# Transposing q and k by DMA instead of on TensorE, in a fused attention and two-MLP kernel

## The chip, the cores and the metric

The kernel runs on one core of one Trainium2 chip. The metric is the device time of one execution in microseconds (us). Each version is timed in several runs; besides, one execution is recorded by the hardware profiler, and the rows below come from that one.

## What is computed

Inputs q, k and v have the shape (4, 8, 576, 64): batch, heads, sequence, head dimension, all float32. Attention is local: each chunk of 64 tokens attends to itself alone. The result, 2304 tokens of 512 features, goes through two MLPs.

```python
q_c = q.reshape(B, H, nc, 64, D)          # the same for k and v, nc = 9
scores = scale * q_c @ k_c^T
attn = exp(scores - max(scores)); attn = attn / (sum(attn) + 1e-9)
x = (attn @ v_c) laid out as (2304, 512)
h = x @ w_in                              # 512 -> 2048
g = max(h, 0) + alpha * min(h, 0)
x = g @ w_out                             # 2048 -> 512
out = ((x @ w_a) * (x @ w_b)) @ w_o       # 512 -> 1536 -> 512
```

The weights arrive as 64-bit floats; the kernel reads them as pairs of 32-bit integers and unpacks them itself. For precision every matmul of the MLPs is done as three, with each operand split into a high and a low float32r part (`three`, L314).

## The kernel before

**Tiles and stages.** The 2304 tokens are 18 units of 128 tokens (a unit is two chunks of all eight heads). They are grouped in five blocks, of 512, 256, 512, 512 and 512 tokens (`sizes`, L52), so units 0 to 3, 4 and 5, 6 to 9, 10 to 13 and 14 to 17. First comes the attention of block 0, in an order written out by hand (`order1`, L584). Then a loop over the blocks (L596) runs the first MLP: 16 hidden steps j per block, each a first-layer product `s1` into a PSUM bank psh, three passes of ScalarE and two of VectorE for the PReLU and the split (`prelu`), and a second-layer product `s2` into four accumulators acc. The second-layer product of a step is issued two steps later (`pend`, `flush(2)`). In block 0 the weights of the first MLP are also loaded, unpacked and split, a few units of work ahead (`prelu_unpacking`, L354; `w_dma`, L174). In the last block the weights of the second MLP follow. Then comes the second MLP over all blocks (L642).

**Attention under the MLP.** While block b goes through the first MLP, the attention of block b+1 is computed, in steps that `att_steps` (L459) returns as pairs (slot, step). Each hidden step has two slots: 2j comes behind the first-layer product, 2j+1 behind the second-layer product that is then due. `advance` (L600) runs all steps whose slot has come. All engines work through their instructions in the order in which they are issued.

For one unit the steps are:
- `load_qk` and `load_v` (L210, L214): DMAs on SP's queue that bring q, k and v with tokens on partitions, into tiles of the pool wp (72 tiles of 128x512; the split weights of the first MLP hold 64 of them).
- `att_T` (L227): four 128x128 transposes of k and four of q on TensorE into two PSUM banks psT, and two evictions by ScalarE into kT and qT (L234).
- `att_S` (L237): the scores, 32 small matmuls; `att_M` (L251): maximum and subtraction on VectorE.
- `soften`: exponential on ScalarE (L266), the sums and the division on VectorE (L268).
- `att_PT` (L277): four transposes of the softmax into psP, and an eviction by ScalarE.
- `att_O` (L286): the product with v, 32 small matmuls, split by ScalarE and VectorE into the next block's xh and xl.

For the blocks of four units, the steps are turn(w), multiply(w), soften(w) in turn, spread evenly over the slots 0 to 29: turn at 0, 7, 14, 21, 27, multiply at 3, 9, 16, 23, 29, soften at 5, 12, 18, 25. A turn transposes q and k of unit w, starts the loads of the next unit's q and k, and transposes the softmax of unit w-1. A multiply does the scores of unit w and the v product of unit w-1. For block 1 (units 4 and 5, under block 0) the slots are written out (L516).

**Shared buffers.** PSUM has four banks for psh, psT, psP, scores and v products together (`ps_p`), and four accumulators. The pool sp, three buffers with the tag stg, holds raw weights, and the tiles in which finished blocks go to and come back from DRAM (xs, xr).

Of the kernel before, what the change touches and what calls it, by code (L numbers as in the profile page):

```python
# [8 lines left out]
F32 = mybir.dt.float32  # L9
F32R = mybir.dt.float32r  # L10
I32 = mybir.dt.int32
U16 = mybir.dt.uint16
AF = mybir.ActivationFunctionType
# [5 lines left out]
def chunk_attention_prelu_mlp_bilinear_mlp(  # L19
# [17 lines left out]
    nc = tc.nc  # L37
    P = 128
    B, H, S, D = q.shape
    NT, DM = out.shape  # L40
# [5 lines left out]
    KD = DM // P  # L46
    J1 = F1 // P
    J2 = F2 // P
    NB = 512
    SCALE = 1.0 / float(D) ** 0.5  # L50

    sizes = [NB] + ([NT % NB] if NT % NB else []) + [NB] * (NT // NB - 1)  # L52
# [9 lines left out]
    sp = ctx.enter_context(tc.tile_pool(name="sp", bufs=3))  # L62
    st = ctx.enter_context(tc.tile_pool(name="st", bufs=4))
    dr = ctx.enter_context(tc.tile_pool(name="dr", bufs=1, space=bass.MemoryType.DRAM))
# [3 lines left out]
    def bank(nm="ps"):  # L68
        return ps_p.tile([P, DM], F32, tag="ps", name=nm)
# [5 lines left out]
    def wtile(name, dt=F32R):  # L75
        return wp.tile([P, DM], dt, tag="w", name=name)
# [88 lines left out]
    def weave(*chains):  # L165


        live, later = [], [iter(c) for c in chains]
        while live or later:
            if later:  # L170
                live.append(later.pop(0))
            live = [c for c in live if next(c, None) is not None]
# [16 lines left out]
    att = {}  # L189

    def runs(t, n):
        done = 0
        while done < n:
            b, s = divmod(t + done, S)
            step = min(n - done, S - s)
            yield done, step, b, s
            done += step

    def half(i):
        return slice(i * CH, (i + 1) * CH)  # L200

    def load(nm, u):
        a = att[nm, u] = wtile(f"{nm}{u}", F32)
        for off, n, b, s in runs(u * P, P):
            nc.sync.dma_start(
                out=a[off:off + n].rearrange("p (h d) -> p h d", h=H),
                in_={"q": q, "k": k, "v": v}[nm][b, :, s:s + n, :].rearrange("h p d -> p h d"),
            )

    def load_qk(u):  # L210
        load("k", u)
        load("q", u)

    def load_v(u):  # L214
        load("v", u)

    n_early = [0]

    def att_bank(u, nm):

        if u < sizes[0] // P:
            n_early[0] += 1
            if n_early[0] % 2:
                return acc_p.tile([P, DM], F32, tag="acc", name=nm)
        return bank(nm)

    def att_T(u, nms="kq"):  # L227
        for nm in nms:
            src = att.pop((nm, u))
            ps = att_bank(u, "psT")  # L230
            for g in range(KD):
                nc.tensor.transpose(ps[:, g * P:(g + 1) * P], src[:, g * P:(g + 1) * P], ident)  # L232
            t = wtile(f"{nm}T{u}", F32)
            nc.scalar.activation(out=t, in_=ps, func=AF.Copy)  # L234
            att[nm + "T", u] = lambda r, g, c, t=t: t[r, half(2 * g + c)]

    def att_S(u, pss=None):  # L237
        qT, kT = att.pop(("qT", u)), att.pop(("kT", u))
        pss = pss or [att_bank(u, "psS") for _ in range(2)]
        for y in range(2):  # L240
            for c in range(2):
                for e in range(2):
                    for x in (e, 1 - e):
                        i = half(e), 2 * x + y, c
                        nc.tensor.matmul(  # L245
                            out=pss[e][half(x), half(2 * y + c)], lhsT=qT(*i), rhs=kT(*i),
                            start=True, stop=True,
                        )
        att["s", u] = pss
# [15 lines left out]
    def att_X(u):  # L265
        nc.scalar.activation(out=att["e", u], in_=att["e", u], func=AF.Exp, scale=SCALE)  # L266
# [10 lines left out]
    def att_PT(u):  # L277
        e_ = att.pop(("e", u))
        ps = att_bank(u, "psP")
        for g in range(KD):  # L280
            nc.tensor.transpose(ps[:, g * P:(g + 1) * P], e_[:, g * P:(g + 1) * P], ident)  # L281
        t = wtile(f"eT{u}", F32)
        nc.scalar.activation(out=t, in_=ps, func=AF.Copy)  # L283
        att["eT", u] = t

    def att_O(u, xh, xl, col, pss=None):  # L286
        eT, v_ = att.pop(("eT", u)), att.pop(("v", u))
        pss = pss or [att_bank(u, "psO") for _ in range(2)]
        for g in range(KD):
            x, y = divmod(g, 2)  # L290
            for c in range(2):
                for e in (c, 1 - c):
                    nc.tensor.matmul(  # L293
                        out=pss[c][half(e), half(g)], lhsT=v_[half(c), half(2 * g + e)],
                        rhs=eT[half(c), half(4 * e + 2 * y + x)], start=True, stop=True,
                    )
        cols = [slice(col + c * CH, col + (c + 1) * CH) for c in range(2)]
        return [
            (xh[:, :, f], xl[:, :, f], ps[:, :KD * CH].rearrange("p (g i) -> p g i", g=KD))
            for f, ps in zip(cols, pss)  # L300
        ]

    def each(fn, parts):
        for part in parts:
            fn(*part)


    def xtiles(nm):
        return (
            xp.tile([P, KD, NB], F32R, tag="xh", name=nm + "h"),  # L310
            xp.tile([P, KD, NB], F32R, tag="xl", name=nm + "l"),
        )
# [138 lines left out]
    NU = NT // P  # L451
# [7 lines left out]
    def att_steps(b, x):  # L459

        t0, n = blocks[b]
        us = range(t0 // P, (t0 + n) // P)

        def turn(w):
            for u in us[w:w + 1]:
                att_T(u)
                if u + 1 < NU:
                    load_qk(u + 1)  # L470
            for u in us[max(w - 1, 0):w]:
                att_PT(u)
            return lambda: None

        def multiply(w):
            pss = [bank("psSO") for _ in range(2)]
            now, before = us[w:w + 1], us[max(w - 1, 0):w]
            for u in now:
                att_S(u, [ps[:, :KD * CH] for ps in pss])
            o = []  # L480
            for u in before:
                o += att_O(u, *x, u * P - t0, [ps[:, KD * CH:] for ps in pss])
                if u + 2 < NU:
                    load_v(u + 2)
            each(to_hi, o)

            def then():
                for u in now:
                    att_M(u)
                each(to_lo, o)  # L490

            return then

        def soften(u):
            att_X(u)
            return lambda: weave(att_N(u))

        def both(product):
            pss = [bank("psSO") for _ in range(2)]
            return [product(u, [ps[:, i * KD * CH:(i + 1) * KD * CH] for ps in pss]) for i, u in enumerate(us)]  # L500

        def both_S():
            both(att_S)
            return lambda: att_M(us[0])

        def both_O():
            o = sum(both(lambda u, pss: att_O(u, *x, u * P - t0, pss)), [])
            each(to_hi, o)
            for u in us:
                load_v(u + 2)  # L510
            return lambda: each(to_lo, o)

        def only(fn):
            return lambda: fn() and None or (lambda: None)

        if b == 1:  # L516
            u0, u1 = us
            return [
                (8, only(lambda: att_T(u0))),
                (10, only(lambda: (att_T(u1), load_qk(u1 + 1)))),  # L520
                (14, both_S),
                (16, lambda: lambda: att_M(u1)),
                (18, lambda: soften(u0)),
                (20, lambda: soften(u1)),
                (24, only(lambda: [att_PT(u) for u in us])),
                (27, both_O),
            ]
        steps = []
        for w in range(len(us) + 1):
            steps += [lambda w=w: turn(w), lambda w=w: multiply(w)]  # L530
            steps += [lambda u=u: soften(u) for u in us[w:w + 1]]
        last = 2 * J1 - 3
        return [(-(-last * i // (len(steps) - 1)), s) for i, s in enumerate(steps)]

    with tc.manual_schedule():
        n0 = sizes[0] // P
# [12 lines left out]
        x = xtiles("x")  # L549
# [46 lines left out]
        for b, (t0, n) in enumerate(blocks):  # L596
            nxt = xtiles("x")
            steps = att_steps(b + 1, nxt) if b + 1 < NBLK else []
# [11 lines left out]
            for j in range(J1):  # L610
# [5 lines left out]
                h = h0[0][:, :n] if not (b or j) else s1(j, x, n)  # L616
                if b == 0:
                    g = prelu_unpacking(j, h, lambda: w_dma(min(2 * j + 9, NU1)), lambda: advance(2 * j), settle)
                else:
                    rest = advance(2 * j)  # L620
                    g = prelu(j, h)
# [17 lines left out]
            x = nxt  # L639
        flush(0)  # L640

        for i, b in enumerate(order2):  # L642
            n = sizes[b]
            for j in range(J2):
                want = NU1 + max(3 * (j + 2), 20 + 2 * j)
                c = s3(j, x, n)
# [14 lines left out]
                if i + 1 < NBLK:  # L661
                    if j == J2 - 3:
                        nxt = xtiles("y")
                        halves = list(reload(order2[i + 1]))
# [3 lines left out]
            x = nxt  # L668
# [31 lines left out]
```

## Time and profile before

| what | value |
|---|---|
| runs, median | 912.65 us |
| runs, lowest and highest | 912.55, 913.15 us |
| the profiled execution's own time | 912.5 us |
| its span in the profile | 910.7 us |
| mean granted TensorE clock | 0.996 of full |
| TensorE (matmul) busy | 898.5 us, 99% |
| VectorE busy | 403.3 us, 44% |
| ScalarE busy | 339.4 us, 37% |

The span is the time from the first to the last recorded instruction; the rest of the profiled execution's time, 1.8 us, lies around it. Matmuls are pipelined and their recorded ends are modelled: two matmuls in a row overlap in the record, so what one costs is read from start to start. A row of the timeline is the start, the duration, the engine, the line of the kernel, the operation, the output and inputs by the program's names, the shape and the count.

### The profile page before, as it was taken

Reading aid. Unit: us, or ns where it says so; the run is one execution under the profiler, and the core shown is the slowest. Engines: PE = TensorE matmul, PEld = TensorE weight load, DVE = VectorE, ACT = ScalarE, POOL = GpSimd, SP = SyncE. Lnnn points to the kernel's source line nnn. Section 1 sums busy time; section 2 is a strip of 40 time slices with the busy share of each in tenths; the row PEclk is TensorE's granted clock in tenths of the full one; section 3 lists DMA queues with packets and bytes.
Section 4 is the critical chain, followed back from the end, with each engine's and each line's share of the span. In section 5 each row is a group of like instructions: output and inputs, shape, how many; then the busy total and the mean of one; then the engine's idle time right before and its main releaser. Section 6 shows DMA issues by size and latency. Waiting matters only on the chain.

```text
span 910.7 us, 13047 instructions
## 1 busy us (share of the span) xinstructions
PE 898.5 (99%) x5426; PEld 756.9 (83%) x5426; DVE 403.3 (44%) x762; ACT 339.4 (37%) x636; POOL 0.7 (0%) x6
## 2 busy tenths in 40 slices
PE   7999999999999999999999999999999999999998
PEld 6878899988888888888888888888888888888897
DVE  5999955443444343368856653111221122111222
ACT  5677654443433343356644432111211122111211
POOL 0000000000000000000000000000000000000000
PEclk9999999999999999999999999999999999999999
DMA  8685432221111110154424420200020002000100
GB/s 209 207 262 179 140 100 52 59 59 35 36 36 59 35 24 2 44 187 139 139 70 140 134 74 13 80 0 1 1 93 1 0 1 70 1 1 0 47 2 23
DMA packets 89098, 62.70 MB, mean 69 GB/s; under 512 B 59856, under 2 KB 81872, under 8 KB 89040
## 3 DMA queue, kind: packets, MB, share of 16 engines
q1 hardware_dynamic: 88752, 61.62, 22.8%
q8 instruction: 42, 0.69, 0.3%
q10 hardware_dynamic: 288, 0.26, 0.1%
q14 instruction: 16, 0.13, 0.1%
HBM read 53.49 MB, written 8.39 MB: 68 GB/s over the span
## 4 chain that ended last, share of the span: by engine, by line
PE 92%; DVE 5%; ACT 2%; issue 1%; POOLq 0%; ACTq 0%; POOL 0%; DVEq 0%
PE psh L317 52%; PE acc L317 36%; PE psT L232 1%; DVE wx L136 1%; PE psSO L245 1%; PE psP L281 1%; PE psSO L293 1%; DVE wz L128 1%; DVE wz L133 1%; DVE gl L82 0%; DVE sm L271 0%; DVE e L275 0%; PE warm L555 0%; DVE e L260 0%; DVE mx L258 0%
## 5 line engine op out<-in xcount | busy, mean ns | idle before, releaser
L393 DVE TENSOR_TENSOR b_sb<-psh,b_sb 128x512 f32<-128x512 f32 (+1 forms) x60 | 38.3, 638 | 273.2 <-PE psh L317 273.2
L337 DVE SCALAR_TENSOR_TENSOR pos<-neg,nalpha_sb,pos 128x512 f32<-128x512 f32 (+1 forms) x80 | 55.6, 695 | 116.4 <-ACT pos L336 116.2
L391 ACT ACTIVATE b_sb<-psh 128x512 f32<-128x512 f32 (+1 forms) x60 | 33.1, 552 | 167.9 <-PE psh L317 167.9
L79 ACT ACTIVATE ch<-b_sb 128x512 fp32r<-128x512 f32 (+1 forms) x60 | 35.3, 589 | 153.9 <-DVE b_sb L393 153.9
L335 ACT ACTIVATE neg<-psh 128x512 f32<-128x512 f32 (+1 forms) x80 | 44.1, 551 | 79.0 <-PE psh L317 79.0
L82 DVE TENSOR_TENSOR gl<-pos,gh 128x512 fp32r<-128x512 f32 (+1 forms) x80 | 51.0, 638 | 43.5 <-ACT gh L79 43.5
L79 ACT ACTIVATE gh<-pos 128x512 fp32r<-128x512 f32 (+1 forms) x80 | 47.3, 591 | 61.5 <-DVE pos L337 61.5
L82 DVE TENSOR_TENSOR cl<-b_sb,ch 128x512 fp32r<-128x512 f32 (+1 forms) x60 | 38.3, 639 | 39.3 <-ACT ch L79 39.3
L136 DVE SCALAR_TENSOR_TENSOR wx<-wx,wz 128x512 int32<-128x512 int32 x68 | 46.8, 688 | 4.9 <-ACT wx L124 1.0
L336 ACT ACTIVATE pos<-psh 128x512 f32<-128x512 f32 (+1 forms) x80 | 44.2, 552 | 0.0
L124 ACT ACTIVATE wx<-raw 128x512 f32<-128x512 f32 x68 | 42.7, 670 | 3.5 <-DMA raw<-in_moe_w_b_dram 3.4
L128 DVE TENSOR_SCALAR wz<-raw 128x512 uint16<-128x512 uint16 x68 | 29.7, 461 | 2.6 <-DMA raw<-in_moe_w_b_dram 2.6
L133 DVE TENSOR_SCALAR wz<-raw 128x512 uint16<-128x512 uint16 x68 | 30.9, 454 | 0.0
L234 ACT ACTIVATE kT<-psT 128x512 f32<-128x512 f32 x18 | 10.7, 594 | 20.1 <-PE psT L232 20.1
L79 ACT ACTIVATE xh<-psSO 128x256 fp32r<-128x256 f32 x28 | 9.1, 381 | 17.1 <-PE psSO L293 17.1
L266 ACT ACTIVATE e<-e 128x512 f32<-128x512 f32 x18 | 11.2, 623 | 10.4 <-DVE e L260 10.4
L281 PE MATMUL psP<-ident,e 128*128 128x128 f32 x72 | 11.6, 287 | 3.3 <-ACT eT L283 1.7
L258 DVE TENSOR_REDUCE mx<-psSO 128x4 f32<-128x256 f32 x28 | 10.5, 416 | 5.2 <-ACT xh L79 5.2
L275 DVE TENSOR_TENSOR e<-e,rc 128x512 f32<-128x512 f32 x18 | 12.4, 691 | 0.6
L271 DVE TENSOR_REDUCE sm<-e 128x8 f32<-128x512 f32 x18 | 12.2, 680 | 1.0 <-ACT e L266 0.8
L281 PEld LDWEIGHTS psP<-ident,e 128*128 128x128 f32 x72 | 8.5, 145 | 4.9 <-ACT eT L283 1.8
L232 PE MATMUL psT<-ident,q 128*128 128x128 f32 x72 | 11.2, 280 | 1.3 <-issue 1.3
(729 smaller groups left out, 2535.4 us busy)
## 6 DMA issues: line engine op xcount, KB each, us to landing
raw<-in_moe_w_out_dram SPq DMA_DIRECT2D x28, 512.0 KB, 3.5
raw<-in_moe_w_in_dram SPq DMA_DIRECT2D x16, 512.0 KB, 4.8
raw<-in_moe_w_b_dram SPq DMA_DIRECT2D x12, 512.0 KB, 4.9
raw<-in_moe_w_a_dram SPq DMA_DIRECT2D x12, 512.0 KB, 3.5
k<-in_k_dram SPq DMA_DIRECT2D x16, 256.0 KB, 3.8
q<-in_q_dram SPq DMA_DIRECT2D x16, 256.0 KB, 3.2
v<-in_v_dram SPq DMA_DIRECT2D x16, 256.0 KB, 3.3
out_dram<-os SPq DMA_DIRECT2D x8, 512.0 KB, 2.8
```

Source lines behind the costliest of these rows:

```text
L79: nc.scalar.activation(out=hi, in_=src, func=AF.Copy)
L82: nc.vector.tensor_tensor(out=lo, in0=src, in1=hi.bitcast(F32), op=ALU.subtract)
L124: return nc.scalar.activation(out=x.bitcast(F32), in_=hw.bitcast(F32), func=AF.Copy, scale=2.0 ** -112)
L128: yield nc.vector.tensor_scalar(out=z2[:, :, 0], in0=h2[:, :, 1], scalar1=13, scalar2=None, op0=ALU.logical_shift_right)
L133: yield nc.vector.tensor_scalar(out=z2[:, :, 1], in0=h2[:, :, 3], scalar1=1 << 15, scalar2=None, op0=ALU.bitwise_and)
L136: yield nc.vector.scalar_tensor_tensor(out=x, in0=x, scalar=3, in1=z, op0=ALU.logical_shift_left, op1=ALU.bitwise_or)
L317: nc.tensor.matmul(out=ps, lhsT=a, rhs=b, start=(i == 0 and first), stop=(i == n_i - 1 and a is wl))
L335: nc.scalar.activation(out=neg, in_=h, func=AF.Relu, scale=-1.0)
L336: yield nc.scalar.activation(out=pos, in_=h, func=AF.Relu)
L337: yield nc.vector.scalar_tensor_tensor(out=pos, in0=neg, scalar=nalpha_sb[:, j:j + 1], in1=pos, op0=ALU.mult, op1=ALU.add)
L391: nc.scalar.activation(out=b_sb, in_=pb, func=AF.Copy)
L393: nc.vector.tensor_tensor(out=b_sb, in0=pa, in1=b_sb, op=ALU.mult)
```

## The change

q and k of units 6 to 17 no longer go through TensorE. Their tiles are loaded as before, but earlier, and mostly into stg buffers (`load_kq`). ScalarE copies each tile as 16-bit integers so that the low and the high halves of all 512 floats are set apart, 512 of each per token (`halves`), and SP stores this to a DRAM tile of 128 tokens x 2 x 512 (`apart`). Then SP issues a transposing DMA, which reads that tile as 256 rows of 512 16-bit elements and writes kT or qT with features on partitions; low and high halves of a float land next to each other, so the result is the float32 tile that the scores read (`turned`, `turn_qk`). The evictions of psT go with the transposes. The even spread of steps is replaced by slots written out for each kind of step: m (multiply), s (soften), p (softmax transposes), l (load), a (apart), t (turn by DMA). One list is for the block of 256 tokens as the running one, the other for 512. In the pairs under l, a and t the second number is the unit counted from the first of the block whose attention is being computed, so 4 and more belong to the block after it. Units 0 to 5 are transposed on TensorE as before.

```diff
+    def load_kq(u, staged=True):
+        att["kq", u] = a = pair(f"kq{u}", staged)
+        for off, n, b, s in runs(u * P, P):
+            for i, src in enumerate((k, q)):
+                nc.sync.dma_start(
+                    out=a[i][off:off + n].rearrange("p (h d) -> p h d", h=H),
+                    in_=src[b, :, s:s + n, :].rearrange("h p d -> p h d"),
+                )
...
+    def halves(src, dst, nm):
+
+        d = dst.bitcast(U16).rearrange("p (t f) -> p t f", t=2)
+        nc.scalar.activation(out=d, in_=src.bitcast(U16).rearrange("p (f t) -> p t f", t=2), func=AF.Copy)
+        rows = dr.tile([P, 2, DM], U16, name=f"rows{nm}")
+        nc.sync.dma_start(out=rows, in_=d)
+        return rows
+
+    def turned(rows, nm):
+        t = wtile(nm, F32)
+        nc.sync.dma_start_transpose(
+            out=t.bitcast(U16).rearrange("p (g r) -> p g r", g=KD), in_=rows.rearrange("p t f -> (p t) f")
+        )
+        return t
+
+    def apart(u, staged=True):
+        a, d = att.pop(("kq", u)), pair("kqd", staged)
+        att["rows", u] = [halves(a[i], d[i], f"{nm}{u}") for i, nm in enumerate("kq")]
+
+    def turn_qk(u):
+        for nm, rows in zip("kq", att.pop(("rows", u))):
+            t = turned(rows, f"{nm}T{u}")
+            att[nm + "T", u] = lambda r, g, c, t=t: t[r, half(2 * g + c)]
...
-        def turn(w):
-            for u in us[w:w + 1]:
-                att_T(u)
-                if u + 1 < NU:
-                    load_qk(u + 1)
-            for u in us[max(w - 1, 0):w]:
-                att_PT(u)
-            return lambda: None
...
         if b == 1:
             u0, u1 = us
             return [
-                (8, only(lambda: att_T(u0))),
-                (10, only(lambda: (att_T(u1), load_qk(u1 + 1)))),
+                (8, only(att_T, u0)),
+                (10, only(att_T, u1)),
+                (10, only(load_kq, u1 + 1, False)),
                 (14, both_S),
                 (16, lambda: lambda: att_M(u1)),
                 (18, lambda: soften(u0)),
                 (20, lambda: soften(u1)),
-                (24, only(lambda: [att_PT(u) for u in us])),
-                (27, both_O),
+                (21, only(apart, u1 + 1, False)),
+                (24, only(att_PT, u0)),
+                (24, only(att_PT, u1)),
+                (24, only(turn_qk, u1 + 1)),
+                (25, only(load_kq, u1 + 2)),
+                (27, lambda: both_O(us)),
+                (28, only(apart, u1 + 2)),
+                (29, only(load_kq, u1 + 3)),
+                (30, only(turn_qk, u1 + 2)),
             ]
-        steps = []
-        for w in range(len(us) + 1):
-            steps += [lambda w=w: turn(w), lambda w=w: multiply(w)]
-            steps += [lambda u=u: soften(u) for u in us[w:w + 1]]
-        last = 2 * J1 - 3
-        return [(-(-last * i // (len(steps) - 1)), s) for i, s in enumerate(steps)]
+        u = us[0]
+        if sizes[b - 1] < NB:
+            S_, lag = {
+                "m": (0, 7, 14, 21, 28), "s": (2, 9, 16, 23), "p": (6, 13, 20, 27),
+                "l": ((4, 3), (11, 4), (18, 5), (29, 6)), "a": ((1, 2), (8, 3), (15, 4), (24, 5)), "t": ((4, 2), (11, 3), (25, 4), (29, 5)),
+            }, 1
+        else:
+            S_, lag = {
+                "m": (0, 6, 12, 18, 28), "s": (2, 8, 14, 20), "p": (5, 11, 17, 27),
+                "l": ((3, 3), (9, 4), (15, 5), (24, 6)), "a": ((1, 2), (7, 3), (15, 4), (23, 5)), "t": ((3, 2), (13, 3), (21, 4), (29, 5)),
+            }, 1
...
```

## Rows read from the trace of the kernel before

**Rows 1.** The page: span, and busy time of each engine
```profile
span 910.7 us, 13047 instructions
...
PE 898.5 (99%) x5426; PEld 756.9 (83%) x5426; DVE 403.3 (44%) x762; ACT 339.4 (37%) x636; POOL 0.7 (0%) x6
```

**Rows 2.** The chain of waits from 110 to 380 us, shares of that stretch by line
```profile
by line: PE psh L317 43.8%; PE acc L317 42.3%; PE psT L232 3.4%; PE psSO L245 2.8%; PE psSO L293 2.3%; PE psP L281 2.1%; issue 0.4%; DVE pos L337 0.4%; ACT gh L79 0.3%; DVE gl L82 0.3%; DVE e L275 0.3%; DVE e L260 0.2%; DVE mx L258 0.2%; AC
```

**Rows 3.** Windows by stage: us, busy us by engine, clock, DMA share, GB/s
```profile
36.00:117.00 81.00, 79.55 (x477) 64.99 (x476) 77.21 (x156) 58.87 (x108) 0.00 (x0) 1.00 0.64 194
117.00:177.60 60.60, 59.98 (x690) 57.24 (x689) 32.16 (x76) 30.30 (x78) 0.00 (x0) 1.00 0.32 77
177.60:273.20 95.60, 95.60 (x690) 79.34 (x690) 38.36 (x74) 39.22 (x75) 0.00 (x0) 1.00 0.17 40
273.20:371.40 98.20, 98.20 (x690) 80.90 (x689) 39.16 (x74) 39.33 (x75) 0.00 (x0) 1.00 0.11 28
```

**Rows 4.** Timeline of TensorE, a turn with k, q and softmax, 512-token stage
```profile
198.28 0.39 PE L317 MATMUL acc<-gh,wo1l 128*128 128x512 f32 x1
198.51 0.60 PE L232 MATMUL psT<-ident,k 128*128 128x128 f32 x4
...
199.74 0.48 PE L317 MATMUL psh<-xh,wi4h 128*128 128x512 f32 x1
```

**Rows 5.** Timeline of TensorE, a turn with the softmax alone, 512-token stage
```profile
260.74 0.39 PE L317 MATMUL acc<-gh,wo11l 128*128 128x512 f32 x1
260.97 0.60 PE L281 MATMUL psP<-ident,e 128*128 128x128 f32 x4
261.32 0.48 PE L317 MATMUL psh<-xh,wi14h 128*128 128x512 f32 x1
```

**Rows 6.** Timeline of TensorE, a turn with k and q alone, 512-token stage
```profile
275.69 0.39 PE L317 MATMUL psh<-xh,wi0l 128*128 128x512 f32 x1
...
276.71 0.48 PE L317 MATMUL acc<-gh,wo14h 128*128 128x512 f32 x1
277.02 0.40 PE L317 MATMUL acc<-gl,wo14h 128*128 128x512 f32 x1
```

**Rows 7.** Timeline of TensorE, three turns in the 256-token stage
```profile
132.70 0.28 PE L317 MATMUL acc<-gh,wo1l 128*128 128x256 f32 x1
...
134.05 0.36 PE L317 MATMUL psh<-xh,wi4h 128*128 128x256 f32 x1
...
145.37 0.28 PE L317 MATMUL psh<-xh,wi7l 128*128 128x256 f32 x1
...
146.86 0.63 PE L281 MATMUL psP<-ident,e 128*128 128x128 f32 x4 [0.34 <-ACT kT L234]
147.24 0.36 PE L317 MATMUL acc<-gh,wo5h 128*128 128x256 f32 x1
...
170.24 0.28 PE L317 MATMUL acc<-gh,wo11l 128*128 128x256 f32 x1
...
170.89 0.36 PE L317 MATMUL psh<-xh,wi14h 128*128 128x256 f32 x1
```

**Rows 8.** Groups of ScalarE instructions, shapes apart: count, busy us, mean ns, idle before
```profile
L124 ACT ACTIVATE wx<-raw 128x512 f32<-128x512 f32 x68 | 42.7, 670 | 3.5 <-DMA raw<-in_moe_w_b_dram 3.4
...
L234 ACT ACTIVATE kT<-psT 128x512 f32<-128x512 f32 x18 | 10.7, 594 | 20.1 <-PE psT L232 20.1
...
L79 ACT ACTIVATE yh<-xr 128x1024 fp32r<-128x1024 f32 x6 | 6.3, 1044 | 0.0
```

**Rows 9.** DMA issues by line: count, KB each, median us to landing
```profile
x2d<-xs SPq DMA_DIRECT2D x2, 256.0 KB, 2.3
xr<-x2d SPq DMA_DIRECT2D x2, 256.0 KB, 3.9
```

**Rows 10.** DMA queue of SP: packets, MB, share of 16 engines
```profile
q1 hardware_dynamic: 88752, 61.62, 22.8%
```

**Rows 11.** Timeline of SP's DMA issues near the end of the first block
```profile
97.99 6.59 SPq L100 DMA_DIRECT2D raw<-in_moe_w_out_dram  x3
```

More of the change, by code (lines that the diff above doesn't have):

```diff
@@ L212, in load_qk, with pair @@
         load("q", u)
+    def pair(nm, staged):
+        if not staged:
+            return [wtile(nm, F32) for _ in range(2)]
+        a = sp.tile([P, 2, DM], F32, tag="stg", name=nm)
+        return [a[:, i] for i in range(2)]
+    def load_kq(u, staged=True):
[6 more added lines that the diff above has]
+                )
     def load_v(u):
         load("v", u)
+    def halves(src, dst, nm):
[17 more added lines that the diff above has]
+            att[nm + "T", u] = lambda r, g, c, t=t: t[r, half(2 * g + c)]
     n_early = [0]
@@ L464, in att_steps, with multiply @@
         us = range(t0 // P, (t0 + n) // P)
-        def turn(w):
-            for u in us[w:w + 1]:
-                att_T(u)
-                if u + 1 < NU:
-                    load_qk(u + 1)
-            for u in us[max(w - 1, 0):w]:
-                att_PT(u)
-            return lambda: None
-        def multiply(w):
+        def multiply(w, lag):
             pss = [bank("psSO") for _ in range(2)]
-            now, before = us[w:w + 1], us[max(w - 1, 0):w]
+            now, before = us[w:w + 1], us[max(w - lag, 0):max(w - lag + 1, 0)]
             for u in now:
@@ L496, in soften, with both @@
             return lambda: weave(att_N(u))
-        def both(product):
+        def both(product, us):
             pss = [bank("psSO") for _ in range(2)]
@@ L502, in both_S, with both_O, nothing, only @@
         def both_S():
-            both(att_S)
+            both(att_S, us)
             return lambda: att_M(us[0])
-        def both_O():
-            o = sum(both(lambda u, pss: att_O(u, *x, u * P - t0, pss)), [])
+        def both_O(us):
+            o = sum(both(lambda u, pss: att_O(u, *x, u * P - t0, pss), us), [])
             each(to_hi, o)
             for u in us:
-                load_v(u + 2)
+                if u + 2 < NU:
+                    load_v(u + 2)
             return lambda: each(to_lo, o)
-        def only(fn):
-            return lambda: fn() and None or (lambda: None)
+        def nothing():
+            pass
+        def only(fn, *a):
+            def step():
+                if a[0] < NU:
+                    fn(*a)
+                return nothing
+            return step
         if b == 1:
@@ L524, in att_steps @@
                 (20, lambda: soften(u1)),
-                (24, only(lambda: [att_PT(u) for u in us])),
-                (27, both_O),
-            ]
-        steps = []
-        for w in range(len(us) + 1):
-            steps += [lambda w=w: turn(w), lambda w=w: multiply(w)]
-            steps += [lambda u=u: soften(u) for u in us[w:w + 1]]
-        last = 2 * J1 - 3
-        return [(-(-last * i // (len(steps) - 1)), s) for i, s in enumerate(steps)]
+                (21, only(apart, u1 + 1, False)),
[7 more added lines that the diff above has]
+                (30, only(turn_qk, u1 + 2)),
+            ]
+        u = us[0]
[9 more added lines that the diff above has]
+            }, 1
+        steps = [(slot, lambda w=w: multiply(w, lag)) for w, slot in enumerate(S_["m"])]
+        steps += [(slot, lambda w=w: soften(us[w])) for w, slot in enumerate(S_["s"])]
+        steps += [(slot, only(att_PT, us[w])) for w, slot in enumerate(S_["p"])]
+        for i, fn in enumerate((load_kq, apart, turn_qk)):
+            steps += [(slot, only(fn, u + n)) for slot, n in S_["lat"[i]]]
+        return sorted(steps, key=lambda s: s[0])
     with tc.manual_schedule():
```

## The prediction, made before the changed kernel ran

> **What bounds the kernel now.** I read the page's busy times first: TensorE is busy for 99% of the span, VectorE and ScalarE under half of it [rows 1]. A matmul's end is modelled, so this alone proves little. The chain of waits does more: cut to the stretch in which the touched attention work lies, it is nearly all TensorE, with the psT transposes on it at 3.4%, and VectorE and ScalarE at tenths of a per cent [rows 2]. The windows by stage say the same: behind the first block TensorE is never idle for long, ScalarE works about 40 to 50% of the time and VectorE as much [rows 3]. In the first block it is otherwise: VectorE is busy 77.2 of 81.0 us there and ScalarE 58.9. So time taken out of TensorE's stream in the three later stages should come off the end, and what is added elsewhere is free until TensorE has to wait for it.
>
> **What the change takes out of TensorE's stream.** For each of the units 6 to 17 the eight 128x128 transposes of k and q go. How long each takes is read from starts, since the durations overlap. In a 512-token stage the step in which k, q and the softmax (psP) are transposed runs from the last acc matmul at 198.28 to the next psh matmul at 199.74: 1.46 us [rows 4]. The same step with psP alone, which is what the change leaves, takes 260.74 to 261.32: 0.58 us [rows 5]. The difference is 0.88 us. Where a stage opens with k and q alone, 275.69 to 276.71 is 1.02 us, less the 0.23 that one matmul takes there anyway (the spacing in rows 4 and 5 of undisturbed 512-column matmuls, seen as 0.23 from 198.28 to 198.51), so 0.79; the next matmul follows after 0.31 in place of 0.23, so 0.87 goes in all [rows 6]. In the 256-token stage the psP step alone is 170.24 to 170.89, 0.65 us; with k and q it is 1.35 us (132.70 to 134.05), and, where psP also waited for a bank that kT's eviction had to free, 1.87 us (145.37 to 147.24) [rows 7]. So 0.70 there and 1.22 where it waited; the third such step waited as well, for the softmax itself, and I take 1.2. The last wait should not come back: before, psP came two slots behind the softmax steps, after, three or four.
> The sum: stage of 256 tokens, 0.87 + 0.70 + 1.22 + 1.20 = 4.0 us; two stages of 512, each 0.87 + 3 x 0.88 = 3.5 us. Together **11.0 us**. As a cross-check, 3.4% of the 270 us of [rows 2] is 9.2 us, without the changeovers and the two waits.
>
> **What stays, and what moves.** Scores, softmax, psP and the products with v are issued as often as before. Their slots move by three at most (a slot is half a hidden step: 2.9 us in the first block, 81.0 / 28, since its slots 4 to 31 lie in that window, 1.9 in the 256-token stage, 60.6 / 32, and 3.0 in the others [rows 3]). The psP eviction still has a slot between it and the product that reads it, at the least 1.9 us against one eviction of 0.59 (kT's, of the same shape [rows 8]). The last product moves from slot 29 to 28, so the next block's input is no later. I cost all this at nothing; its cover is TensorE's own stream, and if that fails the price is the wait of 0.3 us seen in [rows 7], a few times over. PSUM gets easier, since two banks per unit aren't asked for.
>
> **ScalarE.** Two evictions of 0.594 us per unit go; two copies over 1024 16-bit elements per partition come. No row shows a 16-bit copy of that form. The nearest are the 128x1024 f32 copies, 1.04 us [rows 8]; the bounds are 0.6 (as if 512 elements) and 1.3 (twice the longest 512-wide row, 0.67). At 1.04 ScalarE gains 0.9 us per unit, 11 us over 12 units, in stages where it idles for half the time or more [rows 3]. A pair holds the three prelu passes behind it on ScalarE's queue for 2.1 us, and so the psh bank; the second-layer product that reads them comes two hidden steps later, four slots, 7.6 us in the narrow stage and 12 in the wide ones. Nothing, then. In the first block two pairs come (units 6 and 7), where ScalarE is busy for 73%: 4.2 us spread over two steps of 5.8, with the same two steps as cover. Nothing again, but the cover is thinner.
>
> **The SP queue.** Per unit come two stores of 256 KB and two transposing loads of 256 KB; k and q loads move to a unit or more earlier, into the shared staging buffers. The store's row is the 256 KB x2d store, 2.3 us, and for a load out of the kernel's own DRAM tile the 256 KB xr load, 3.9 us [rows 9]. A transposing DMA stands in no row. Low end: 2.3 us. High end: if every 16-bit element were a packet of its own, 131072 packets at the queue's mean of 37 ns (22.8% of 16 x 910.7 us over 88752 packets [rows 10]) over 16 engines, 306 us each. I take 3.9, because the xr row is the same queue, the same direction, the same bytes and the same kind of source; so **7.8 us a pair** if they run one behind the other. The queue waits for ScalarE's copies at the stores, and for the stores at the transposes; behind it stand the next k, q and v loads, which have a unit's time.
> What matters is the lead from issue to the scores that read the pair, counted in slots: 20 us for unit 6 (seven slots of 2.9 to the block's end), 16 for 7 (one such, and seven of 1.89), 19 for 8 and 9 (ten of 1.89), 13.2 for 10 (slot 25 to the next stage's start, seven of 1.89), 15 for 13 and 17 (five of 3.0), over 20 for the rest. 7.8 us is under all of them, so the transposes cost nothing: the sum stays at 11.0.
> A row says 3.9 us for this size. The Trainium skill, "VectorE: DVE Perf Modes", The three transpose paths, gives 1309 ns for the DMA crossbar on one 128x128 block of 16-bit data; a tile here has eight such blocks, by my estimate 10.5 us and 21 us a pair if they follow one another, which would not be hidden and would make the whole about 19 us slower than before. The Trainium skill, "DMA: Bandwidth & Descriptors", Latency and other measured facts, has 261 GB/s for a transposing DMA, an estimated 1.0 us per tile, which would leave the sum as it is. No run shown here decides between them.
>
> **The rivals.**
> Slow transposes, the one on the other side: each takes 10 us or more, some 2.6 times the xr row, so 20 us a pair. Then the scores wait where the lead is short: unit 10 for 6.8 us, 13 and 17 for 5 each, 7 for 4, 8 and 9 for 1.1 each, in all 23 us, which less 11.0 ends at 912.5 + 12 = **924.5 us**. It decides from about 17.5 us a pair on, where these waits reach 11 us. For it: the operation is unseen, and a store must land before it. Against it: the rings are used for 11 to 32% of the time there [rows 3]. The Trainium skill's 1309 ns (VectorE: DVE Perf Modes, The three transpose paths) speaks for it too.
> A jam at the end of the first block: unit 6's transposes stand on the queue just ahead of the last raw weights (three w_out and w_in loads around 98 to 105 us, already spaced by waits [rows 11]), and its copies want two more working tiles when the weight tiles fill the pool. Unpacking is in order on engines that are 73 to 95% busy there [rows 3]. If the raw tiles come some 16 us late (two pairs at 7.8) against two steps of cover, 11.6 us, about 5 us of the gain goes: **906.5 us**.
> No gain: the freed time is refilled by waits of the same size on moved steps or late copies, or the change doesn't in fact take the transposes off TensorE's path: **912.5 us**. For it: only the change of slots, which no row prices. Against it: the chain.
>
> **How the numbers follow.** The profiled execution took 912.5 us, 0.15 under the median of the runs; 912.5 - 11.0 = **901.5 us**. Forecast 0.67, its own range 899 to 904.5 (the missing waits and a cheaper changeover one way, a few waits of 0.3 us and one bank held by ScalarE the other). Jam 0.12, slow transposes 0.16, no gain 0.05. The range of 8 in 10 runs from 899 to 911, over the forecast and the jam; the slow case and the no gain case are left out with two in ten. 0.2% is 1.8 us, about what this measurement can tell from no change. Faster: forecast and jam, 0.79; same: most of the no gain case, 0.04; slower: the slow transposes and the rest, 0.17.
>
> **What the profile after would show.** Right: psT transposes 24 each of k and q (units 0 to 5) in place of 72; no L232 work after 120 us; the 256-token stage 4 us shorter, each of the two after it 3.5 us; no wait of TensorE for a DMA-written kT or qT; ScalarE's copies near 1.04 us; transposes landing in 3 to 5 us. Wrong: scores that wait for kT or qT, above all units 10, 13 and 17 (slow transposes); ScalarE or VectorE waiting for raw, or the first block longer than before (jam); stages as long as before with new releasers in TensorE's waits (no gain). The prediction falls if a transposing DMA takes over some 8.5 us, or if ScalarE's copy takes several times 1.04.

## The result and the profile after

The changed kernel takes **901.57 us** (901.50 to 901.70), the kernel before, timed alongside it, 912.60: a ratio of 0.9878, 95% interval 0.9866 to 0.9891, or 11.0 us less.

The page after: busy time of each engine. TensorE is still at 99%, of a span of 899.7 us, and ScalarE has grown by 10.5 us (339.4 in [rows 1]).

```profile
PE 889.1 (99%) x5330; PEld 747.5 (83%) x5330; DVE 402.7 (45%) x762; ACT 349.9 (39%) x636; POOL 0.7 (0%) x6
```

The windows by stage after (us of the window, busy us and count for TensorE, its weight loads, VectorE, ScalarE, GpSimd, then granted clock, DMA share, GB/s). The stages are cut at the first psh matmul of each block, as in [rows 3].

```profile
36.00:117.04 81.04, 80.05 (x479) 65.40 (x479) 77.34 (x156) 62.53 (x112) 0.00 (x0) 1.00 0.74 216
117.04:173.14 56.10, 56.10 (x658) 53.95 (x657) 32.00 (x76) 33.41 (x77) 0.00 (x0) 1.00 0.71 171
173.14:265.73 92.59, 92.46 (x658) 75.73 (x657) 38.03 (x74) 42.84 (x75) 0.00 (x0) 1.00 0.39 89
265.73:360.41 94.68, 94.68 (x658) 77.45 (x656) 38.92 (x74) 39.17 (x71) 0.00 (x0) 1.00 0.18 45
```

So the first block takes 81.0 us as before, the 256-token stage 56.1 in place of 60.6, the 512-token stages 92.6 in place of 95.6 and 94.7 in place of 98.2: 4.5 + 3.0 + 3.5 = 11.0 us. In each of the three TensorE is busy for all or nearly all of the window, with 32 matmul records less.

The chain of waits from 110 to 370 us, shares by line. psT, at 3.4% in [rows 2], is gone from it, and neither kT nor qT nor a DMA has come in; the steps of VectorE and ScalarE are at 0.6% or less.

```profile
by line: PE acc L362 45.3%; PE psh L362 43.7%; PE psSO L290 2.6%; PE psSO L338 2.3%; PE psP L326 2.0%; issue 0.6%; DVE pos L382 0.6%; ACT gh L79 0.5%; ACT neg L380 0.5%; ACT pos L381 0.4%; DVE mx L303 0.3%; DVE gl L82 0.3%; DVE e L305 0.3%;
```

The timeline of TensorE around a softmax transpose in the 256-token stage, after: 166.01 to 166.48 is 0.47 us, and psP begins 0.12 us behind the matmul before it.

```profile
166.01 0.28 PE L362 MATMUL acc<-gh,wo11l 128*128 128x256 f32 x1
166.13 0.60 PE L326 MATMUL psP<-ident,e 128*128 128x128 f32 x4
166.48 0.36 PE L362 MATMUL psh<-xh,wi14h 128*128 128x256 f32 x1
```

Before, the step with psP alone took 0.65 us, from 170.24 to 170.89, and psP began 0.26 us behind the matmul at 170.24; with k and q the steps took 1.35 or 1.87 [rows 7].

```profile
170.50 0.63 PE L281 MATMUL psP<-ident,e 128*128 128x128 f32 x4
```

ScalarE's copies, then the DMA issues by line (count, KB each where given, median us to landing):

```profile
L241 ACT ACTIVATE kqd<-kq 128x1024 uint16<-128x1024 uint16 x24 | 23.9, 1046 | 0.3 <-DMA kq<-in_k_dram 0.3
```

```profile
rowsk<-kqd SPq DMA_DIRECT2D x12, 256.0 KB, 2.0
rowsq<-kqd SPq DMA_DIRECT2D x12, 256.0 KB, 2.1
...
kT<-rowsk SPq DMA_TRANSPOSE x12, 4.0
qT<-rowsq SPq DMA_TRANSPOSE x12, 3.8
```

A copy takes 1.046 us, as the 128x1024 f32 copies of [rows 8] do; the stores land in 2.0 and 2.1 us (2.3 in [rows 9]) and the transposing DMAs in 4.0 and 3.8 us (3.9 for the xr load in [rows 9]). SP's issues (start, us held, line) show what no row of before could: a transposing DMA holds SP's queue for 1.2 us or more.

```profile
118.39 1.59 SPq L248 DMA_TRANSPOSE kT<-rowsk  x1
120.09 1.24 SPq L248 DMA_TRANSPOSE qT<-rowsq  x1
```

From the first issue to the second landing this pair takes, by the median landing, 120.09 + 3.8 - 118.39 = 5.5 us.

### The profile page after: what moved, and what is told of

It is laid out like the page before. It is cut to its first block, busy times and chain, and to the rows that moved or that the text cites. A ratio compares the mean times of both kernels' runs of the same rounds, so it can differ in the third digit from the quotient of the medians.

```text
span 899.7 us, 12924 instructions
## 1 busy us (share of the span) xinstructions
PE 889.1 (99%) x5330; PEld 747.5 (83%) x5330; DVE 402.7 (45%) x762; ACT 349.9 (39%) x636; POOL 0.7 (0%) x6
## 4 chain that ended last, share of the span: by engine, by line
PE 89%; DVE 7%; ACT 2%; issue 1%; DMA 1%; SPq 0%; ACTq 0%; DVEq 0%
PE psh L362 51%; PE acc L362 36%; DVE wx L136 1%; DVE wz L128 1%; PE psSO L338 1%; PE psP L326 1%; DVE wz L133 1%; PE psSO L290 1%; DVE gl L82 1%; DMA k<-in_k_dram 0%; DVE sm L316 0%; DMA raw<-in_moe_w_in_dram 0%; DVE mx L303 0%; DVE e L305 0%; DVE e L320 0%
## 5 line engine op out<-in xcount | busy, mean ns | idle before, releaser
L241 ACT ACTIVATE kqd<-kq 128x1024 uint16<-128x1024 uint16 x24 | 23.9, 1046 | 0.3 <-DMA kq<-in_k_dram 0.3
L326 PE MATMUL psP<-ident,e 128*128 128x128 f32 x72 | 11.8, 290 | 2.6 <-ACT eT L328 1.7
L328 ACT ACTIVATE eT<-psP 128x512 f32<-128x512 f32 x18 | 10.6, 598 | 7.8 <-PE psP L326 7.8
L82 DVE TENSOR_TENSOR xl<-psSO,xh 128x256 fp32r<-128x256 f32 x28 | 10.4, 414 | 1.5 <-ACT xh L79 1.5
```

Source lines behind the costliest of these rows:

```text
L82: nc.vector.tensor_tensor(out=lo, in0=src, in1=hi.bitcast(F32), op=ALU.subtract)
```

## The experiments

**The slots without the DMA.** q and k go back to TensorE, at the slots of the transposing DMAs; the copies (`apart`) do nothing.

```diff
...
     def turn_qk(u):
-        for nm, rows in zip("kq", att.pop(("rows", u))):
-            t = turned(rows, f"{nm}T{u}")
...
+        for nm, a in zip("kq", att.pop(("kq", u))):
+            att[nm, u] = a
+        att_T(u)
```

> The changed kernel's slots and staged loads, but with the eight transposes of k and q of units 6 to 17 back on TensorE, at the slots of the transposing DMAs; no copies, no stores, no transposing DMAs. Theory (the whole gain is TensorE's stream): twelve times 0.87 us come back on 901.6, so 912.0 us, between 911 and 913. Rival (a good part of the gain is the new slots): 910 us or less.

Measured: 921.61 us, ratio 1.0096 [1.0079, 1.0113]. A miss of 9.6 us. The windows of the first block and of the three later stages together, and TensorE's wait (us in all, times, longest), say where.

```profile
36.00:126.87 90.87, 83.67 (x494) 68.34 (x492) 79.71 (x159) 62.89 (x115) 0.00 (x0) 0.96 0.64 185
126.87:380.49 253.62, 252.62 (x2050) 215.66 (x2048) 106.91 (x221) 105.48 (x218) 0.00 (x0) 1.00 0.16 40
```

```profile
PE psT L276 <- ACT pos L380: 6.4, 2, 5.5
```

The three later stages take 253.6 us against 243.4 after the change and 254.4 before: 10.2 us come back there, as expected. The rest is the first block, 90.9 us: unit 6's transposes stand at slot 24 behind the softmax transposes of units 4 and 5 and wait up to 5.5 us for a PSUM bank that ScalarE holds; part of the rest of the 9.9 us is matmuls at a lower granted clock, 0.96 on average over the block. That is this experiment's own slot, so it was moved.

> The changed kernel's slots for scores, softmax and softmax transposes; q and k of all units transposed on TensorE, in one step with the softmax transposes as in the kernel before (the first unit of each later block at slot 29 of the stage before), loads as before, nothing by DMA. Theory (the whole gain is TensorE's stream, and the first run's extra 9.8 us in the first block came from the slot at which it transposed unit 6): the first block is as long as before, 81 us, and the time is 911 to 914 us, the kernel before's, with short waits in the 256-token stage where scores follow the transposes by one slot. Rival (the new slots gain or cost by themselves): under 910 or over 916 us.

```diff
-                (24, only(turn_qk, u1 + 1)),
...
+                (29, only(T_load, u1 + 1)),
...
+        steps += [(slot, only(T_load, us[w + 1])) for w, slot in enumerate(S_["p"][:3])]
+        steps += [(29, only(T_load, u + 4))]
...
```

(`T_load` is `att_T(u)` and the loads of the next unit.) Measured: 917.11 us, ratio 1.0045 [1.0030, 1.0060]; over the range given. The same two windows:

```profile
36.00:120.64 84.64, 81.17 (x488) 66.20 (x486) 78.62 (x158) 61.72 (x113) 0.00 (x0) 1.00 0.65 192
120.64:374.59 253.95, 253.33 (x2058) 216.79 (x2056) 107.35 (x222) 105.89 (x221) 0.00 (x0) 1.00 0.17 42
```

Again the three later stages are nearly the kernel before's (254.4): 254.0 us, 10.6 above the changed kernel's, where twelve times 0.87 is 10.4. And again the first block is longer, by 3.6 us, with unit 6's transposes waiting 2.5 us for a bank. So the slots alone bring 0.4 to 0.8 us in the later stages; TensorE's freed stream brings the rest. That the first block must stay clear of unit 6's transposes on TensorE was not foreseen; what the kernel before did, at the opening of the next stage, cost less.

**Is anything of the added work still paid for?** This kernel leaves out the copies, the stores and the transposing; a plain load fills kT and qT.

```diff
     def turn_qk(u):
...
+        ts = [wtile(f"{nm}T{u}", F32) for nm in "kq"]
+        load_plain(u, ts)
...
```

> Left out: ScalarE's copies, the stores and the transposing; kT and qT of units 6 to 17 are filled by a plain load of k and q (untransposed) at the slots of the transposing DMAs, so the scores of these units are of the wrong numbers. Theory (all that the change adds is hidden but for the 0.3 to 0.4 us waits seen in the second wide block): 901.1 to 901.7 us. Rival (the copies or the added DMA traffic hold TensorE somewhere unseen): under 900.5 us.

Measured: 901.66 us, ratio 0.9880 [0.9866, 0.9895]. The stages:

```profile
117.27:173.36 56.09, 56.09 (x658) 53.94 (x656) 31.85 (x76) 26.34 (x69) 0.00 (x0) 1.00 0.31 77
173.36:265.90 92.54, 92.41 (x659) 75.74 (x657) 38.03 (x74) 35.18 (x67) 0.00 (x0) 1.00 0.17 41
265.90:360.58 94.68, 94.68 (x658) 77.46 (x656) 38.92 (x74) 35.39 (x67) 0.00 (x0) 1.00 0.11 29
```

56.09, 92.54 and 94.68 us, with the copies, stores and transposes in place 56.10, 92.59 and 94.68. All that the change adds is hidden to within 0.1 us, though ScalarE does 22 us less here and the DMA engines move less than half as much in the narrow stage (77 GB/s against 171). The narrow stage is the one of 256 tokens; the wide ones are the two of 512.

**How far does the cover reach?** Each transposing DMA was issued twice and three times (`for _ in range(2)` around the issue in `turned`).

> Each transposing DMA is issued twice into the same tile, so a pair takes 16 us if each waits for the one before (four of 4.0 us, as they landed after the change). By the leads of the prediction (13.2 us for unit 10, 15 for units 13 and 17) scores then wait about 3 us at unit 10 and 1 us each at 13 and 17: 901.6 + 5 = 906.5 us, between 903 and 910. If the four overlap, so that the pair takes 8 us or less: 901.6 us. Rival (the leads are longer than slots say, or shorter): no wait at all with pairs over 14 us, or over 912 us.

> Each transposing DMA is issued three times into the same tile: 24 us a pair if they follow one another. By the leads of the prediction the scores wait 11 us at unit 10, 9 each at 13 and 17, 8 at 7, 5 each at 8 and 9, 4 at 6: about 50 us, less what one wait gives the next unit, so 930 to 950 us, and the waits of TensorE name kT and qT. Rival (the transposes are hidden whatever they take): 901.6 us.

Measured: 915.97 us for two (914.55 to 916.91, ratio 1.0035 [1.0023, 1.0046]) and 967.6 us for three, from one run and so without an interval. Both cost more than expected. Windows, TensorE's and ScalarE's waits, and SP's issues of the kernel with two:

```profile
36.00:122.37 86.37, 81.92 (x480) 66.28 (x478) 76.52 (x155) 61.24 (x111) 0.00 (x0) 0.98 0.72 207
122.37:187.33 64.96, 58.78 (x657) 55.56 (x656) 33.20 (x78) 34.56 (x79) 0.00 (x0) 0.97 0.69 163
187.33:279.87 92.54, 92.47 (x658) 75.77 (x657) 38.02 (x74) 42.87 (x75) 0.00 (x0) 1.00 0.62 131
279.87:374.55 94.68, 94.68 (x657) 77.45 (x656) 38.91 (x74) 39.18 (x71) 0.00 (x0) 1.00 0.24 56
```

```profile
PE psSO L291 <- DMA qT<-rowsq: 4.7, 2, 3.3
PE acc L363 <- ACT gh L79: 2.6, 1, 2.6
```

```profile
ACT wx L124 <- DMA raw<-in_moe_w_out_dram: 7.0, 1, 7.0
```

```profile
100.19 6.62 SPq L249 DMA_TRANSPOSE kT<-rowsk  x2
...
111.55 0.53 SPq L100 DMA_DIRECT2D raw<-in_moe_w_out_dram  x1
...
141.69 7.22 SPq L249 DMA_TRANSPOSE kT<-rowsk  x2
148.95 4.56 SPq L249 DMA_TRANSPOSE qT<-rowsq  x2
```

The first block has grown by 5.3 us, the 256-token stage by 8.9, the wide stages not at all. In the first block the last raw weight load is issued at 111.55, behind unit 6's four transposes; ScalarE waits 7.0 us for it, and TensorE 2.6 us for the gh that stands behind that wait. This is the jam that the prediction named, at its place. In the narrow stage the waits are for qT, of units 8 and 9, not 10: the queue was still working off unit 7's (to 135.07) when unit 8's turn came, and behind them stood stores and loads, so that unit 8's were issued at 141.69 only, and a pair takes 148.95 + 4.56 - 141.69 = 11.8 us on SP alone, 12 to 15 us with the last landing. Units 13 and 17, for which a wait was expected as well, have none. With three, TensorE's longest waits are the same two, larger:

```profile
PE psSO L291 <- DMA qT<-rowsq: 33.7, 6, 8.4
PE acc L363 <- ACT gh L79: 10.5, 1, 10.5
```

To test the order on the queue, unit 6's doubled pair was put behind the last raw load (slot 25 for 24).

> Each transposing DMA issued twice, as before, but unit 6's pair moved from slot 24 to 25, behind the last raw weight load on SP's queue. Theory (5.3 of the 14.4 us that the doubling cost were the last raw weights standing behind unit 6's transposes, ScalarE waiting 7.0 us for them): the wait of ScalarE for raw goes, the first block is 81 to 82 us again, and the time is 910 to 912 us. Rival (the first block suffers from the DMA traffic, not from the order on the queue): 915 us or more.

Measured: 915.06 us (913.12 to 917.42), ratio 1.0025 [1.0015, 1.0035].

```profile
36.00:116.93 80.93, 79.51 (x477) 65.01 (x476) 77.16 (x156) 60.37 (x109) 0.00 (x0) 1.00 0.71 206
116.93:184.90 67.97, 59.50 (x657) 56.09 (x656) 31.97 (x76) 35.67 (x79) 0.00 (x0) 0.95 0.75 174
```

The first block is back at 80.9 us with the DMA engines as busy as before (0.71 against 0.72), so the order on the queue made the jam. The time did not fall to 911 all the same, and by the time alone the rival came in: the narrow stage is 68.0 us in place of 65.0. The jam has moved to the next load on the queue: k and q of unit 7 are now issued behind unit 6's four transposes, at 116.33; ScalarE, whose copy of them stands ahead of a gh, waits 5.8 us, and TensorE 3.8 us for that gh. (Lines of SP, ScalarE and TensorE.)

```profile
116.33 0.52 SPq L225 DMA_DIRECT2D kq<-in_k_dram  x1
120.35 2.00 ACT L241 ACTIVATE kqd<-kq 128x1024 uint16<-128x1024 uint16 x2 [5.78 <-DMA kq<-in_k_dram]
122.92 0.80 PE L363 MATMUL acc<-gh,wo14h 128*128 128x512 f32 x1 [3.77 <-ACT gh L79]
```

The waits for qT did not grow: 3.4 us in two, against 4.7. The windows are those of one execution each, of 913.2 us here and 915.6 with unit 6's pair at slot 24; the runs of the two kernels overlap.

**The same on ScalarE.** Every copy was made twice, then only those of units 12 to 17.

> Each of ScalarE's 16-bit copies is made twice into the same tile: 24 more at 1.05 us, 25 us more of ScalarE's time. Theory (ScalarE's part is hidden behind TensorE with two steps of cover): 901.6 to 902.5 us. Rival (the held psh banks and the prelu queue make ScalarE's copies cost at least half their time): 907 us or more, 914 if all of it.

> ScalarE's copies made twice only for units 12 to 17, whose copies lie in the 512-token stages: 12 more, 12.6 us. Theory (the 14 us that doubling all copies cost came from the copies of the 256-token stage and its start, where 4.2 us in one piece outlast the cover; a hidden step of 6 us covers them): 901.6 to 902.3 us. Rival (ScalarE's time costs the same share everywhere): 901.6 + 7 = 908 us.

Measured: 915.45 us (ratio 1.0029 [1.0020, 1.0039]) and 903.41 us (0.9900 [0.9887, 0.9914]). The narrow and the first wide stage with every copy twice, the chain in that narrow stage, and the wide stages with the copies of units 12 to 17 twice:

```profile
117.97:184.83 66.86, 60.77 (x657) 56.80 (x656) 33.06 (x78) 44.45 (x88) 0.00 (x0) 0.95 0.58 142
184.83:279.24 94.41, 92.71 (x659) 75.67 (x658) 37.91 (x75) 50.52 (x83) 0.00 (x0) 1.00 0.41 90
```

```profile
by line: ACT kqd L242 27.6%; DVE pos L383 8.0%; DMA kq<-in_k_dram 7.9%; PE acc L363 7.7%; issue 6.7%; ACT gh L79 5.4%; PE psh L363 5.0%; ACT neg L381 3.6%; ACT pos L382 3.5%; ACT e L312 3.1%; PE psSO L339 2.9%; DVE sm L317 2.7%; DVE gl L82 
```

```profile
173.18:267.60 94.42, 92.70 (x659) 75.66 (x657) 37.95 (x74) 50.50 (x83) 0.00 (x0) 1.00 0.40 89
267.60:362.28 94.68, 94.68 (x657) 77.38 (x656) 38.74 (x74) 43.02 (x75) 0.00 (x0) 1.00 0.19 45
```

The rival of the first came in at more than half: of 25 us added to ScalarE 13.9 are paid for (its 914 us, given for all of them, is the price of half). 10.8 of them are in the narrow stage, where the copies now make up 27.6% of the chain. TensorE is idle there for 6.1 us, and its matmuls take 4.7 us more (60.8 for 56.1), at a granted clock of 0.95 on average. Its waits name the softmax (2.3 us), the copies out of the accumulators (1.2) and the eviction of the softmax (0.8), all of which stand behind the copies on ScalarE or behind what waits for them, and only once a gh (1.4). In the wide stages 12.6 us more cost 1.8, all of it in the first of them (94.42 for 92.59 us), where TensorE waits 1.7 us for the copies out of the accumulators, and nothing in the last, which has two of the six pairs. So ScalarE's share of the change is free at its size, and in the narrow stage not at twice its size.

**Two more units.** Units 4 and 5 by DMA as well.

```diff
-                (8, only(att_T, u0)),
-                (10, only(att_T, u1)),
...
+                (5, only(apart, u0, False)),
+                (8, only(turn_qk, u0)),
+                (9, only(apart, u1, False)),
...
+                (11, only(turn_qk, u1)),
...
```

> Units 4 and 5 too are transposed by DMA, in the first block (copies at slots 5 and 9, transposes at 8 and 11, scores at 14 as before). Theory (TensorE's stream sets the first block as well, since it works 80 of its 81 us): two units at 0.87 us, 901.6 - 1.7 = 899.9 us. Rival (VectorE and ScalarE, busy 77 and 63 of 81 us there, or raw weights held up on SP's queue set the first block): 901.6 us or more.

Measured: 912.91 us (910.80 to 915.61), ratio 1.0003 [0.9994, 1.0012]: the rival, and more. The profiled execution took 910.8, and its first block 90.4 us. Unit 5's copy on ScalarE, the load of raw w_out ahead of its transposes and the second transpose on SP, TensorE's scores, and a window of the first block:

```profile
59.99 1.99 ACT L241 ACTIVATE kqd<-kq 128x1024 uint16<-128x1024 uint16 x2
64.45 3.35 SPq L100 DMA_DIRECT2D raw<-in_moe_w_out_dram  x1
70.18 2.33 SPq L248 DMA_TRANSPOSE qT<-rowsq  x1
75.19 1.13 PE L290 MATMUL psSO<-kT,qT 64*64 64x64 f32 x32 [9.97 <-DMA qT<-rowsq]
```

```profile
72.00:80.00 8.00, 4.81 (x42) 3.97 (x43) 6.55 (x14) 5.05 (x9) 0.00 (x0) 0.53 1.09 298
```

The scores wait 10.0 us for unit 5's qT. ScalarE, in order behind unpacking, ended the copies only at 61.98, 3.2 us before TensorE came to those scores at 65.22. Then the load of raw w_out held SP's queue for 3.35 us (such loads wait 10.8 us in four stops between 30 and 80 us, for buffers that VectorE's unpacking frees), and qT landed 5.0 us after its issue, with the 16 DMA engines busy all the time (DMA share 1.09). So the held load is a part of the wait and the late copy another; no run takes them apart. From 72 us, in that wait, to 80 us TensorE's granted clock averages 0.53 of full: nearly all of that at the lower of its two levels, 1.2 GHz, after TensorE had done nothing since 65.2.

**The wait that the moved steps brought.** In the first wide stage TensorE pauses in a second-layer product: 186.18 to 186.70 is 0.52 us in place of 0.23 (timeline of the changed kernel, with VectorE's copy out of the accumulators):

```profile
186.18 0.39 PE L362 MATMUL acc<-gh,wo0l 128*128 128x512 f32 x1
186.70 0.50 PE L362 MATMUL acc<-gh,wo0h 128*128 128x512 f32 x1
186.23 0.75 DVE L455 COPY xs<-acc 128x256 f32<-128x256 f32 x2
```

> The first softmax step of a 512-token stage at slot 3 in place of 2, behind the copies out of the accumulators. Theory (in the changed kernel the second-layer product of the second 512-token... of the first 512-token stage waits 0.3 us, with a slow restart 0.4, for an accumulator whose copy to xs stands behind that softmax's sums on VectorE): that wait goes, 901.2 us, between 901.0 and 901.4. Rival (the 0.45 us that this stage saved less than forecast comes from elsewhere): 901.6 us.

Measured: 901.47 us (901.15 to 901.83), ratio 0.9877 [0.9863, 0.9890]. The wide stage's window:

```profile
173.70:265.84 92.14, 92.14 (x658) 75.81 (x657) 38.04 (x75) 42.74 (x75) 0.00 (x0) 1.00 0.41 90
```

92.14 us in place of 92.59: the wait is gone and its cause shown. The whole time can't be told from the changed kernel's, as the first block of the profiled run was 0.6 us longer.

**A version that beats both.** In the wide stages the softmax is transposed by DMA too, and the product with v comes one multiply later.

```diff
+    def apart_e(u):
+        att["rows_e", u] = halves(att.pop(("e", u)), wtile("ed", F32), f"e{u}")
+    def turn_e(u):
+        att["eT", u] = turned(att.pop(("rows_e", u)), f"eT{u}")
...
-                "m": (0, 6, 12, 18, 28), "s": (2, 8, 14, 20), "p": (5, 11, 17, 27),
+                "m": (0, 6, 12, 18, 24, 29), "s": (3, 8, 14, 20), "p": (), "ae": (4, 9, 15, 21), "te": (6, 11, 17, 24),
...
-            }, 1
+            }, 2
...
```

> In the two 512-token stages (units 10 to 17) the softmax too is transposed by DMA: ScalarE sets its halves apart (slots 4, 9, 15, 21), SP stores them and transposes them (6, 11, 17, 24), and the product with v comes two multiplies later in place of one; the first softmax at slot 3. Theory (what leaves TensorE's stream comes off the end as long as its result has a lead of some 8 us): eight psP steps at 0.58 us, 4.6 us, and the 0.4 us of the accumulator's wait: 896.6 us, between 896 and 898. Rival (SP's queue, which now holds three stores and three transposes per unit, brings kT, qT or eT late): over 901.6 us, and TensorE's waits name them.

Measured: **898.40 us** (897.87 to 898.86), ratio 0.9843 [0.9830, 0.9857], 3.2 us under the changed kernel. The two wide stages, and the landing of the new transposes:

```profile
173.59:264.14 90.55, 90.55 (x643) 74.24 (x641) 38.21 (x74) 44.34 (x75) 0.00 (x0) 1.00 0.47 114
264.14:357.23 93.09, 93.09 (x641) 75.89 (x640) 39.01 (x74) 40.64 (x71) 0.00 (x0) 1.00 0.26 69
```

```profile
eT<-rowse SPq DMA_TRANSPOSE x8, 3.3
```

90.6 and 93.1 us, 2.0 (0.45 of it the accumulator's wait) and 1.6 less than after the change, with no wait of TensorE that names a transposed tile. Each stage was expected to lose 2.3 us and more. The 0.58 us per psP step was the wrong price: of it, 0.23 is the matmul that is there anyway [rows 5], so four steps are worth 1.4 us; and one step of scores and product together, 1.41 us, has become two apart of 0.94 each, which costs 0.24 after the same deduction. That makes 1.2 of the 1.6 us. The matmul behind a step is slower too (0.31 in place of 0.23 us in [rows 6]), an estimated 0.2 for the three steps saved in all; the rest stays open.

## Why the prediction was right

- **TensorE's stream, 11.0 us.** Forecast 4.0, 3.5 and 3.5 us for the three stages, measured 4.5, 3.0 and 3.5. That the stages' difference is the removed transposes, and not the slots, is shown by the two kernels with the slots alone, whose later stages are 10.2 and 10.6 us longer than the changed kernel's. The narrow stage gained half a microsecond more: the 0.65 us that the sum took for psP alone was itself a step with a late start, and all four such steps take 0.47 or 0.48 us after, 0.7 us less in all; the opening gave some 0.2 less than its 0.87.
- **Moved steps at nothing.** One was not nothing: the softmax moved ahead of the accumulator's copies on VectorE and cost 0.45 us in the first wide stage. It and the narrow stage's surplus cancel, so that the sum came out better than its terms: the mechanism was right, the agreement to 0.1 us is luck.
- **ScalarE at 1.04 us a copy.** Measured 1.046; hidden, as said. The reason given, a cover of two hidden steps (7.6 us) in the narrow stage, counted only the PReLU passes behind the copies: at 4.2 us a pair TensorE waited 1.4 us for a gh, but 4.3 us for softmax and accumulator steps, for which no cover was worked out.
- **The transposing DMA at 3.9 us.** Measured 4.0 and 3.8, and 5.5 us a pair in place of 7.8. The Trainium skill's 1309 ns per 128x128 block (VectorE: DVE Perf Modes, The three transpose paths), taken eight times, would be 10.5 us by estimate: the trace does not agree for a tile of eight blocks, which lands in 4.0 us. The Trainium skill's 261 GB/s, given there for a non-contiguous middle dimension (DMA: Bandwidth & Descriptors, Latency and other measured facts), would be 1.0 us by estimate; the runs show only the time from issue to landing, so it is neither shown nor refuted.
- **The leads.** They held, since 5.5 us is far below all of them. But counting slots to the scores was a poor measure of the margin. The prediction put the break-even at 17.5 us a pair, at units 10, 13 and 17; with 12 to 15 us a pair the kernel was already 3.4 us slower than before, at units 6, 8 and 9. What counts is the order on SP's queue: raw weights, stores and loads wait behind a transpose, and the next pair behind the last.
- **The rivals.** Slow transposes did not happen, and neither did the jam; both are real mechanisms, which twice the transposes brought out. The rival of no gain is ruled out by the stages.

## What to carry to other kernels

Where one engine's stream is the whole chain, the price of an operation is the start-to-start difference of two steps with and without it in the same stage, and that difference is what comes off the end; the step without it must itself start on time, and the matmul that is there anyway must not be counted. The work that replaces it on other queues needs its margin counted per queue and in order (what stands ahead, what waits behind), not from issue to use; the stage with the shortest steps and the stage that still loads weights have the least. A step moved in an instruction list must be checked against what it now precedes on every engine it uses.

## What the runs showed of the hardware

A transposing DMA of 256 KB lands as fast as a plain load of the same size out of DRAM (3.8 to 4.0 us against 3.9), but holds SP's queue about three times as long at issue (1.2 us at the least against 0.36 for a store of that size). The copy of 1024 16-bit elements with a stride of two takes ScalarE as long as one of 1024 floats (1.046 and 1.044 us [rows 8]). Some of the slower kernels scatter: 910.8 to 915.6 us with units 4 and 5 by DMA and 913.1 to 917.4 with unit 6's doubled pair moved, in ten runs each, against 0.2 us in four runs of the changed kernel. Waits of TensorE for DMAs alone don't account for it: with every copy made twice, where no wait of TensorE names a DMA, ten runs spread over 3.0 us.
